# The memory term of an attention kernel as 64 more keys of its last score block

## The chip, the cores and the metric

The kernel runs on one core of one Trainium2 chip. The metric is the device time of the run in microseconds (us). Three runs of the kernel before took 566.57, 567.1 and 568.01 us, median 567.1. The engines are TensorE (PE, with its weight loads as PEld), VectorE (DVE), ScalarE (ACT), GpSimd (POOL) and SyncE (SP), which issues all DMAs here.

## The reference

For 4 batches, 8 heads, 576 positions and 64 channels, all in float32:

```
a     = exp(s - max(s)) / (sum + 1e-9),  s = q k^T / 8, causal
local = a v
phi(x) = max(x, 0) + exp(min(x, 0))
mem   = phi(q) M_prev / (phi(q) . z_prev + 1e-6)
out   = g * mem + (1 - g) * local,       g = sigmoid(beta), per head
x     = out as 2304 rows of 512
y     = ((x w1) * (x w2)) w3 w_out
```

Since nothing stands between w3 and w_out, the kernel multiplies these two once and uses their product.

## The kernel before, in words

The work goes by **pairs**: two heads (a = 0, 1) of one batch, 16 pairs in all, four to a batch. The 576 queries of a head are cut into five chunks: chunk 0 has 64 queries (those of both heads share one tile, `sm0`), chunks 1 to 4 have 128 each, for 64 + 128 c keys (`KE`). The scores of a chunk are a tile `sm{a}{c}` of 128 queries by `KE[c]` keys and 64 columns of zeros, so that whole blocks of 128 columns can be transposed.

A pair passes through these steps (names are the functions; lines are those of the profile):

- `s_all`, `s_mm0` (L205, L191): scores on TensorE; `s_red` (L182) on VectorE adds the mask and takes the maximum; `s_exp` (L215) on ScalarE; `s_norm` (L219 to L224) on VectorE divides by the sum and by the gate's part (1 - g, in `gis`).
- `t_mm` (L234, L255): transposes of the score blocks on TensorE into a PSUM bank `s`, copied by ScalarE into `pt` (L265). The groups are called 1, 2, h, 3a, 3b, 4a, 4b, 5.
- The memory term: `mem_a` (L138, L139, ScalarE) and `mem_b` (L144, VectorE) build phi(q) in the tile `qn`; GpSimd multiplies it by z (L146), VectorE sums over channels and makes n = g / sum (L151 to L157), GpSimd scales phi(q) by n (L159). `mem_t` (L165) transposes the five blocks and ScalarE copies them to `mt` (L167). `mem_mm` (L271, L272) multiplies `mt` by the memory matrix of both heads, which stand as diagonal blocks in `md`, into the PSUM tile `x`.
- `pv_mm` (L281): transposed scores times v are added to the same `x`; the two heads write the lower and the upper 64 partitions. v is five blocks of 128 keys; the last one holds 64 keys and 64 zeros.
- `fin` (L292, L293): `x` leaves PSUM as a high part and a remainder, the input of the MoE products.

Float32 matmuls stand in the trace as two records each.

Beside the pairs runs a **fill**: TensorE work that is cut into small steps and dealt out evenly over the F marks of the string `ORDER`, which also gives the order of a pair's steps. In batch 0 the fill is the product of w3 and w_out (L427), in batches 1 to 3 the MoE products of the batch before (`gemm1` L477, with L483 to L489 behind it; `gemm2` L497), and after the last pair those of the last batch, alone. The weights come as 64-bit floats; ScalarE and VectorE convert them in 40 jobs (`conv_tick`, L314 to L327): the first 24 are w_out and w3, the last 16 are w1 and w2 (`wp`, `wsp`). Their loads are `wst<-w_out`, `wst<-w3t` and `wst<-w`.

All loads are issued by SP in program order, and a DMA waits for the eighth DMA before it to land. The framework reorders instructions of an engine by priority before the program is built, so the order on an engine is not that of the code.

Of the kernel before, what the change touches and what calls it, by code (L numbers as in the profile page):

```python
# [13 lines left out]
ALU = mybir.AluOpType  # L14
# [7 lines left out]
    "lv mt t1 c c F "  # L22
# [3 lines left out]
    "t4b t5 F "  # L26
    "mm pv ma F "
# [15 lines left out]
def attention_moe_kernel(  # L43
# [22 lines left out]
    PT = 1920  # L66
# [27 lines left out]
    sm = [[None] + [const.tile([128, KE[c] + 64], F32, name=f"sm{a}{c}") for c in range(1, 5)] for a in range(2)]  # L94
    qd = const.tile([128, 128], F32, name="qd")
    md = const.tile([128, NC, 128], F32, name="md")
# [4 lines left out]
    raw_t, v_t, qn_t, z_t, mt_t, pt_t, sums_t, stat = ({} for _ in range(8))  # L101
# [13 lines left out]
    def load_v(p):  # L115
        b, h = heads(p)
        t = v_t[p] = v_p.tile([128, 2, 5, D], F32, tag="v", name="v")
        for a in range(2):
            nc.sync.dma_start(out=t[:, a], in_=v[b, h + a])

    def load_qn(p):
        b, h = heads(p)
        t = mem_p.tile([128, 5, 2, D], F32, tag="qn", name="qn")
        nc.sync.dma_start(out=t, in_=qn[b, h // 2])
        zt = z_p.tile([128, 2, D], F32, tag="z", name="z")
        zs = z_prev[b, h:h + 2]
        nc.sync.dma_start(out=zt, in_=bass.AP(tensor=zs.tensor, offset=zs.offset, ap=[[0, 128], [D, 2], [1, D]]))
        qn_t[p], z_t[p] = t, zt

    def load_m(b):  # L130
        src = m_prev[b].rearrange("d (j t) e -> d t j e", t=2)
        for a in range(2):
            nc.sync.dma_start(out=md[64 * a:64 * a + 64, :, 64 * a:64 * a + 64], in_=src[:, a])

    def mem_a(p):
        t = qn_t[p]
        e = mem_p.tile([128, 5, 2, D], F32, tag="e", name="e")
        nc.scalar.activation(out=e, in_=t, func=ACTF.Relu, scale=-1.0)  # L138
        nc.scalar.activation(out=e, in_=e, func=ACTF.Exp, scale=-1.0)  # L139
        stat["e", p] = e  # L140

    def mem_b(p):
        t, e = qn_t[p], stat["e", p]
        nc.vector.scalar_tensor_tensor(out=t, in0=t, scalar=0.0, in1=e, op0=ALU.max, op1=ALU.add)  # L144
        zb = z_t.pop(p).rearrange("p (o h) d -> p o h d", o=1).to_broadcast([128, 5, 2, D])
        nc.gpsimd.tensor_tensor(out=e, in0=t, in1=zb, op=ALU.mult)  # L146

    def mem_c(p):
        t, e = qn_t[p], stat.pop(("e", p))
        n = st_p.tile([128, 10, 1], F32, tag="n", name="n")  # L150
# [80 lines left out]
    def t_mm(p, what):  # L231
# [3 lines left out]
        if what in ("4a", "4b", "3a", "3b"):  # L235
# [28 lines left out]
        for s, d in jobs:
            nc.scalar.activation(out=d, in_=s, func=ACTF.Copy)  # L265
# [427 lines left out]
```

## Time and profile before

| | us |
|---|---|
| median of three runs (566.57 to 568.01) | 567.1 |
| span of the profiled execution | 564.3 |
| PE busy | 542.7 (96%) |
| PEld busy | 433.6 (77%) |
| DVE busy | 281.2 (50%) |
| ACT busy | 276.7 (49%) |
| POOL busy | 106.7 (19%) |

The span runs from the first to the last instruction of the profiled execution; a run's time has some 2.8 us more around it. Busy shares are means over stages with different limits; in the page's 40 slices VectorE is at 9 tenths in slices 2 and 6, TensorE in nearly all from slice 8 on. A matmul's end is modelled, so starts are the better measure.

### The profile page before, as it was taken

To read this page: it belongs to the slowest core of one execution; us is meant where nothing else is said; L and a number is where in the kernel's file an instruction comes from. 1 tells how busy PE (TensorE), PEld (TensorE's weight loads), DVE (VectorE), ACT (ScalarE), POOL (GpSimd) and SP (SyncE) were. 2 spreads that over 40 slices of the span, in tenths; PEclk is the share of its full clock that TensorE was granted. 3 is DMA by queue.
4 is the path that set the end of the run, shared out by engine and by line. 5 is a ranking of instruction groups with operands and counts; after the bars stand their busy time and mean duration, and the time that the engine had idled before them with its cause. 6 is when DMAs were issued, how large, how long until landed. Compare 5 with 4: busy or idle time off the path is not lost.

```text
span 564.3 us, 9257 instructions
## 1 busy us (share of the span) xinstructions
PE 542.7 (96%) x3440; PEld 433.6 (77%) x3440; DVE 281.2 (50%) x896; ACT 276.7 (49%) x723; POOL 106.7 (19%) x137
## 2 busy tenths in 40 slices
PE   4899989799999999999999999999999999999997
PEld 2344544458896979787978898798969797998995
DVE  6986899759653436263626272624534351111110
ACT  5656775749562637173725464354625361220210
POOL 1101202010430122212230313031301220220210
PEclk9899999999999999999999999999999999999999
DMA  7991646612111202121213021311112000000001
GB/s 294 417 375 51 218 132 224 208 49 94 40 62 44 87 28 69 57 88 30 67 29 106 28 55 35 100 48 39 58 43 88 23 2 20 20 1 37 1 1 56
DMA packets 23068, 48.31 MB, mean 86 GB/s; under 512 B 6896, under 2 KB 13040, under 8 KB 21488
## 3 DMA queue, kind: packets, MB, share of 16 engines
q1 hardware_dynamic: 23024, 47.72, 25.1%
q8 instruction: 27, 0.44, 0.3%
q14 instruction: 17, 0.14, 0.1%
HBM read 43.00 MB, written 4.72 MB: 85 GB/s over the span
## 4 chain that ended last, share of the span: by engine, by line
PE 83%; DVE 8%; ACT 4%; DMA 3%; issue 1%; SPq 0%; POOL 0%; DVEq 0%; ACTq 0%; POOLq 0%
PE m L477 37%; PE m L497 18%; PE s L234 8%; PE x L281 7%; PE s L205 5%; PE m L427 3%; DMA wst<-w 2%; PE x L272 2%; PE sx L205 2%; PE x L165 1%; ACT sm L215 1%; DMA wst<-w_out 1%; DVE sm L224 1%; DVE wsp L327 1%; ACT pt L265 1%; DVE w3s L319 1%
## 5 line engine op out<-in xcount | busy, mean ns | idle before, releaser
L477 PE MATMUL m<-xs,wsp 128*128 128x288 f32 x1536 | 223.5, 299 | 0.0
L477 PEld LDWEIGHTS m<-xs,wsp 128*128 128x128 f32 x1536 | 206.9, 188 | 1.2
L489 POOL TENSOR_TENSOR ht<-a,ht 128x288 fp32r<-128x288 f32 (+2 forms) x96 | 59.0, 628 | 261.6 <-ACT ht L488 242.3
L215 ACT ACTIVATE sm<-sm,mx 128x320 f32<-128x320 f32 (+3 forms) x144 | 82.6, 575 | 45.2 <-DVE mx L182 45.1
L497 PE MATMUL m<-wH,ht 128*128 128x512 f32 x288 | 95.4, 398 | 0.0
L265 ACT ACTIVATE pt<-s 128x512 f32<-128x512 f32 (+1 forms) x144 | 63.8, 497 | 27.7 <-PE s L234 27.4
L486 DVE SCALAR_TENSOR_TENSOR a<-m,a 128x288 f32<-128x288 f32 x64 | 29.2, 456 | 91.7 <-PE m L477 87.4
L427 PE MATMUL m<-wo,w3s 128*128 128x512 f32 x128 | 63.5, 625 | 5.7 <-DVE w3s L319 3.8
L234 PE MATMUL s<-ident,sm 128*128 128x128 f32 x448 | 61.7, 273 | 3.1 <-DVE sm L224 2.9
L497 PEld LDWEIGHTS m<-wH,ht 128*128 128x128 f32 x288 | 54.1, 188 | 11.5
L234 PEld LDWEIGHTS s<-ident,sm 128*128 128x128 f32 x448 | 52.3, 140 | 10.8 <-DVE sm L224 4.5
L488 ACT ACTIVATE ht<-a 128x288 fp32r<-128x288 f32 (+2 forms) x96 | 31.4, 361 | 56.0 <-DVE a L486 56.0
L182 DVE CUSTOM_DVE_ANT_0 sm<-s,mask 128x320 f32<-128x320 f32 (+3 forms) x112 | 45.7, 448 | 23.1 <-PE s L205 23.1
L497 PE MATMUL m<-wL,ht 128*128 128x512 f32 x144 | 56.2, 390 | 0.0
L224 DVE TENSOR_SCALAR sm<-sm,sums 128x320 f32<-128x320 f32 (+3 forms) x144 | 54.2, 430 | 1.1
L146 POOL TENSOR_TENSOR e<-qn,z 128x640 f32<-128x640 f32 x16 | 25.8, 1612 | 149.0 <-DVE qn L144 149.0
L483 ACT ACTIVATE a<-m 128x288 f32<-128x288 f32 x64 | 26.3, 411 | 47.7 <-PE m L477 42.2
L281 PEld LDWEIGHTS x<-pt,v 128*64 128x64 f32 x384 | 25.0, 137 | 29.9 <-issue 23.3
L281 PE MATMUL x<-pt,v 128*64 128x448 f32 (+4 forms) x384 | 46.7, 392 | 0.0
L293 DVE TENSOR_TENSOR xs<-x,xs 128x576 fp32r<-128x576 f32 x16 | 12.1, 755 | 66.0 <-ACT xs L292 66.0
L427 PEld LDWEIGHTS m<-wo,w3s 128*128 128x128 f32 x128 | 22.8, 197 | 28.1 <-issue 16.6
L205 PE MATMUL s<-raw 64*128 64x320 f32 (+3 forms) x256 | 38.1, 412 | 4.4 <-DMA raw<-qkt 4.4
(65 smaller groups left out, 458.0 us busy)
## 6 DMA issues: line engine op xcount, KB each, us to landing
raw<-qkt SPq DMA_DIRECT2D x16, 576.0 KB, 3.8
wst<-w3t SPq DMA_DIRECT2D x8, 1024.0 KB, 9.0
wst<-w SPq DMA_DIRECT2D x16, 512.0 KB, 4.7
qn<-qn SPq DMA_DIRECT2D x16, 320.0 KB, 3.0
v<-v SPq DMA_DIRECT2D x32, 160.0 KB, 2.3
out<-o SPq DMA_DIRECT2D x18, 256.0 KB, 2.0
wst<-w_out SPq DMA_DIRECT2D x4, 1024.0 KB, 12.1
z<-z_prev SPq DMA_DIRECT2D x16, 64.0 KB, 2.8
```

The lines of the kernel that those rows point to most:

```text
L182: nc.vector.tensor_tensor_reduce(out=sm[a][c][:, lo:hi] if c else sm0[:, 0:64], in0=x, in1=mask[:, S - KE[c] + lo:S - KE[c] + hi] if c els ...
L205: nc.tensor.matmul(y, lhsT=t[r, 0, 128 * c - 64:128 * c + 64], rhs=t[r, 1, lo:hi], start=True, stop=True)
L215: nc.scalar.activation(out=x, in_=x, func=ACTF.Exp, bias=mx, scale=-1.0, accum_out=sums_of(p)[:, k:k + 1])
L224: nc.vector.tensor_scalar(out=x, in0=x, scalar1=sums_of(p)[:, k:k + 1], scalar2=None, op0=ALU.mult)
L234: tr = lambda o, c, a, kc: nc.tensor.transpose(ps[:, o:o + 128], sm[a][c][:, 128 * kc:128 * kc + 128], ident)
L265: nc.scalar.activation(out=d, in_=s, func=ACTF.Copy)
L281: nc.tensor.matmul(x[64 * a:64 * a + 64, 384 + q0:384 + q1], lhsT=vv[:, a, kc], rhs=pt[:, a, o:o + q1 - q0], start=False, stop=(q0 == 0 or ...
L427: nc.tensor.matmul(ps, lhsT=w[:, 128 * kc:128 * kc + 128], rhs=wo[:, 512 * (kc % 2):512 * (kc % 2) + 512], start=(kc == 0), stop=(kc == 7))
L477: nc.tensor.matmul(ps[:, 0:U], lhsT=w[:, i, x, j], rhs=x_t[NC * b + j][:, xx, U * u:U * u + U], start=(k == 0), stop=(k == 11))
L488: nc.scalar.activation(out=hbuf(f, 0)[:, p:p + c], in_=a[:, o:o + c], func=ACTF.Copy)
L489: nc.gpsimd.tensor_tensor(out=hbuf(f, 1)[:, p:p + c], in0=a[:, o:o + c], in1=f32(hbuf(f, 0)[:, p:p + c]), op=ALU.subtract)
L497: nc.tensor.matmul(ps, lhsT=hbuf(f, a)[:, p:p + 128], rhs=b[f], start=(k == 0), stop=(k == 23))
```

## The change

The memory term becomes 64 more keys. Chunk c's last block of 128 score columns had 64 keys and 64 zeros; the zeros are replaced by phi(q) scaled by g / (phi(q) . z + 1e-6), 64 features for each query. v's block for that chunk has 64 rows of v below and the 64 rows of the memory matrix above, so one product adds both terms. As each chunk ends at another key, v gets nine blocks: four whole ones, and five (one for each chunk) of half v and half memory. `mem_t`, `mem_mm`, `load_m` and the tile `md` go; the score tiles of chunks 1 to 4 become slices of one tile `smx`, so that GpSimd can write two chunks of both heads in one instruction. The features are loaded in an order that fits the chunks (`qn` as nine blocks). The transposes are regrouped: 1, 2, h, 3a, 3b, 4a, 4b and s.

```diff
 ORDER = (
-    "lv mt t1 c c F "
+    "lv t1 c c F "
...
-    "t4b t5 F "
-    "mm pv ma F "
+    "t4b ts F "
+    "pv ma F "
...
     def load_v(p):
         b, h = heads(p)
-        t = v_t[p] = v_p.tile([128, 2, 5, D], F32, tag="v", name="v")
-        for a in range(2):
-            nc.sync.dma_start(out=t[:, a], in_=v[b, h + a])
+        t = v_t[p] = v_p.tile([128, 2, 9, D], F32, tag="v", name="v")
+        for a in range(2):
+            nc.sync.dma_start(out=t[:, a, 0:4], in_=v[b, h + a][:, 0:4])
+            nc.sync.dma_start(out=t[0:64, a, 4:9], in_=v[b, h + a][0:64])
+            m = m_prev[b][:, h + a]
+            nc.sync.dma_start(out=t[64:128, a, 4:9], in_=bass.AP(tensor=m.tensor, offset=m.offset, ap=[[DM, D], [0, 5], [1, D]]))
...
     def load_qn(p):
...
-        nc.sync.dma_start(out=t, in_=qn[b, h // 2])
...
+        nc.sync.dma_start(out=t[half[0], 0:8], in_=y[half[1], 0:4].rearrange("p t h d -> p (t h) d"))
+        nc.sync.dma_start(out=t[half[1], 0:8], in_=y[half[0], 1:5].rearrange("p t h d -> p (t h) d"))
+        for a in range(2):
+            nc.sync.dma_start(out=t[half[a], 8], in_=y[half[0], 0, a])
...
     def mem_b(p):
...
-        nc.gpsimd.tensor_tensor(out=e, in0=t, in1=zb, op=ALU.mult)
...
+        nc.gpsimd.tensor_tensor(out=by_pair(e), in0=by_pair(t), in1=zb, op=ALU.mult)
+        nc.gpsimd.tensor_tensor(out=e[:, 8], in0=t[:, 8], in1=zt[:, 2], op=ALU.mult)
...
     def mem_c(p):
...
-        nc.gpsimd.tensor_tensor(out=tv, in0=tv, in1=n.to_broadcast([128, 10, D]), op=ALU.mult)
-
-    def mem_t(p):
-        t = qn_t.pop(p)
-        x = ps_x.tile([128, 1024], F32, tag="x", name="x")
-        for i in range(5):
-            nc.tensor.transpose(x[:, 384 + 128 * i:512 + 128 * i], t[:, i].rearrange("p h d -> p (h d)"), ident)
-        mt = mt_t[p] = mem_p.tile([128, S], F32, tag="mt", name="mt")
-        nc.scalar.activation(out=mt, in_=x[:, 384:960], func=ACTF.Copy)
...
+        nc.gpsimd.tensor_tensor(out=sm0[:, 64:128], in0=t[:, 8], in1=n[:, 8].to_broadcast([128, D]), op=ALU.mult)
+        for k, lo, q in ((0, 0, 384), (4, 512, 640)):
+            d = smx[:, :, lo:lo + 2 * q].rearrange("p a (k q) -> p k a q", q=q)[:, :, :, q // 2 if k == 0 else 576:]
+            d = d[:, :, :, 0:D]
+            by_pair = lambda y: y[:, k:k + 4].rearrange("p (k a) d -> p k a d", a=2)
+            nc.gpsimd.tensor_tensor(out=d, in0=by_pair(t), in1=by_pair(n).to_broadcast([128, 2, 2, D]), op=ALU.mult)
...
+            blocks, lo, st, o = {
+                "1": (((1, 0), (1, 1)), 0, SP[1], 0),
+                "2": (((2, 0), (2, 1)), 0, 384, 128),
+                "s": (((2, 2), (4, 4)), 1024, 384, 256),
+            }[what]
...
-    def mem_mm(p):
-        x = stat["x", p] = ps_x.tile([128, 1024], F32, tag="x", name="x")
-        mt = mt_t.pop(p)
-        lhsT = md[:, p % NC]
-        nc.tensor.matmul(x[:, 384:512], lhsT=lhsT, rhs=mt[:, 0:128], start=True, stop=False)
-        nc.tensor.matmul(x[:, 512:960], lhsT=lhsT, rhs=mt[:, 128:576], start=True, stop=False)
-
     def pv_mm(p):
-        x, pt, vv = stat["x", p], pt_t.pop(p), v_t.pop(p)
-        for kc in range(5):
-            off = 1024 if kc == 4 else 576 * kc
-            for q0, q1 in ((0, 128), (128, 576)) if kc == 0 else ((128 * kc, 576),):
-                for a in range(2):
...
+        x = stat["x", p] = ps_x.tile([128, 1024], F32, tag="x", name="x")
+        pt, vv = pt_t.pop(p), v_t.pop(p)
+        jobs = [(kc, 512 * kc, 128 * kc + 64, 576) for kc in range(4)]
+        jobs += [(4 + c, SP[c], max(128 * c - 64, 0), 128 * c + 64) for c in (1, 2, 3, 4, 0)]
+        for k, o, q0, q1 in jobs:
             for a in range(2):
...
+                nc.tensor.matmul(
+                    x[64 * a:64 * a + 64, X0 + q0:X0 + q1], lhsT=vv[:, a, k], rhs=pt[:, a, o:o + q1 - q0],
+                    start=k in (0, 4), stop=k in (8, 4),
+                )
...
-    for c in range(1, 5):
-        for a in range(2):
-            nc.vector.memset(sm[a][c][:, KE[c]:KE[c] + 64], 0.0)
...
     for b in range(B):
-        load_m(b)
```

The order of the instructions on TensorE, from the last transposes of the first pair of batch 1 to its value products, before (L234 transposes, L477 fill, L271 and L272 memory products, L281 value products):

```order
L477 MATMUL m<-xs,wsp 128x288 x9
L234 MATMUL s<-ident,sm_115 128x128 x4
L234 MATMUL s<-ident,sm_111 128x128
L234 MATMUL s<-ident,sm_115 128x128
L477 MATMUL m<-xs,wsp 128x288 x12
L271 MATMUL x<-mt,md 128x128
L272 MATMUL x<-mt,md 128x448
L281 MATMUL x<-pt,v 64x128 x2
L281 MATMUL x<-pt,v 64x448 x4
L281 MATMUL x<-pt,v 64x320 x2
L281 MATMUL x<-pt,v 64x192 x2
L281 MATMUL x<-pt,v 64x64 x2
```

The same place now (L240 transposes, L468 fill, L272 value products):

```order
L240 MATMUL s<-ident,smx 128x128 x7
L468 MATMUL m<-xs,wsp 128x288 x9
L240 MATMUL s<-ident,smx 128x128 x5
L468 MATMUL m<-xs,wsp 128x288 x12
L272 MATMUL x<-pt,v 64x512 x2
L272 MATMUL x<-pt,v 64x384 x2
L272 MATMUL x<-pt,v 64x256 x2
L272 MATMUL x<-pt,v 64x128 x10
L272 MATMUL x<-pt,v 64x64 x2
```

The value products follow the fill directly, as 18 instructions instead of 12 and two.

SP's queue before, from the features of pair 1 to the second load of w1 and w2:

```order
L124 DMA qn<-qn 128x640
L127 DMA z<-z_prev 128x128
L303 DMA wst<-w 128x1024
L113 DMA qd<-qkt 64x64 x2
L119 DMA v<-v 128x320 x2
L303 DMA wst<-w 128x1024
```

SP's queue now, from pair 1's values to the first two loads of w1 and w2; ahead of the rows stand pair 1's features and pair 2's scores' inputs:

```order
L123 DMA v<-v 128x256
L124 DMA v<-v 64x320
L126 DMA v<-m_prev 64x5x64
L133 DMA qn<-qn 64x512
L134 DMA qn<-qn 64x512
L136 DMA qn<-qn 64x64 x2
L139 DMA z<-z_prev 128x128
L142 DMA z<-z_prev 64x64 x2
L294 DMA wst<-w 128x1024 x2
```

Both weight loads moved behind pair 1's values and pair 2's features.

VectorE before, from the conversion of the first halves of w1 and w2 (`wp`, `wsp`) to the reductions of pair 2's scores (ISA):

```order
L318 TENSOR_SCALAR wp<-wp 128x512
L327 TENSOR_TENSOR wsp<-wp,wsp 128x512
L151 TENSOR_REDUCE n<-e 128x10
L319 SCALAR_TENSOR_TENSOR wp<-wst,wp 128x512
L293 TENSOR_TENSOR xs<-x,xs 128x576
L419 SCALAR_TENSOR_TENSOR wL_129<-m,wH_121 128x512
L182 ISA sm_109,mx<-s,mask 128x320
```

VectorE now, among the same reductions, the first six rows of which stand ahead of these:

```order
L188 ISA smx,mx<-s,mask 128x192
L188 ISA mx 128x1
L164 TENSOR_REDUCE n<-e 128x9
L309 TENSOR_SCALAR wp<-wp 128x512
L165 TENSOR_SCALAR n<-n 128x9
L310 SCALAR_TENSOR_TENSOR wp<-wst,wp 128x512
L188 ISA smx,mx<-s,mask 128x448
```

Two whole conversions stood ahead of pair 2's reductions; now the first one begins between them. Up to pair 3's last normalisation eight of these conversions stood on VectorE, now seven.

## Rows read from the trace of the kernel before

**Rows 1.** Stages: busy us (count) of PE, PEld, DVE, ACT, POOL; clock, DMA.
```profile
core 0: us, PE busy (x) PEld busy (x) DVE busy (x) ACT busy (x) POOL busy (x), PEclk, DMA share, GB/s
...
70.00:90.00 20.00, 17.46 (x82) 9.71 (x82) 19.78 (x60) 16.47 (x41) 2.83 (x2) 1.00 0.53 174
90.00:110.00 20.00, 16.44 (x76) 8.17 (x73) 18.26 (x58) 11.25 (x29) 1.55 (x1) 1.00 0.64 213
...
130.00:564.30 434.30, 430.18 (x2944) 374.51 (x2943) 177.40 (x577) 192.10 (x522) 89.92 (x118) 1.00 0.15 46
```

**Rows 2.** Waits of PE, longest first: us in total, times, longest.
```profile
PE s L205 <- DMA raw<-qkt: 4.4, 1, 4.4
```

**Rows 3.** Timeline of PE: start, us, instruction, idle time before it.
```profile
81.02 1.32 PE L234 MATMUL s<-ident,sm 128*128 128x128 f32 x10 [1.14 <-DVE sm L224]
...
108.56 1.32 PE L234 MATMUL s<-ident,sm 128*128 128x128 f32 x10 [1.75 <-DVE sm L224]
```

**Rows 4.** The chain that ended last: start, us, what; pair 3, then pair 4.
```profile
114.54 0.22 PE x L271 x2
114.77 0.75 PE x L272 x2
115.52 2.85 PE x L281 x24
...
128.69 0.55 PE x L165 x5
```

**Rows 5.** Timeline of PE in narrow windows over one pair's value products.
```profile
200.76 0.33 PE L281 MATMUL x<-pt,v 128*64 128x128 f32 x2
...
200.92 0.66 PE L281 MATMUL x<-pt,v 128*64 128x128 f32 x4
...
202.54 0.44 PE L281 MATMUL x<-pt,v 128*64 128x320 f32 x2
...
203.07 0.50 PE L281 MATMUL x<-pt,v 128*64 128x192 f32 x4
...
203.40 0.28 PE L281 MATMUL x<-pt,v 128*64 128x64 f32 x4
```

**Rows 6.** Groups by line and form: busy us, mean ns, idle before.
```profile
L281 PEld LDWEIGHTS x<-pt,v 128*64 128x64 f32 x384 | 25.0, 137 | 29.9 <-issue 23.3 <-DMA z<-z_prev 1.3 <-DMA wst<-w 0.7
```

**Rows 7.** Timelines of PE and of POOL around one pair's last transposes.
```profile
197.84 0.81 PE L234 MATMUL s<-ident,sm 128*128 128x128 f32 x6
...
195.78 1.56 POOL L146 TENSOR_TENSOR e<-qn,z 128x640 f32<-128x640 f32 x1 [1.62 <-DVE qn L144]
198.95 0.40 POOL L489 TENSOR_TENSOR ht<-a,ht 128x96 fp32r<-128x96 f32 x1 [1.61 <-ACT ht L488]
199.31 1.26 POOL L159 TENSOR_TENSOR qn<-qn,n 128x640 f32<-128x640 f32 x1
```

**Rows 8.** Timeline of SP: issues at the start.
```profile
4.30 0.48 SPq L590 DMA_DIRECT2D beta_sb<-beta  x1
...
7.05 1.30 SPq L388 DMA_DIRECT2D wst<-w_out  x3
```

**Rows 9.** DMA issues: KB each, median us from issue to landing.
```profile
v<-v SPq DMA_DIRECT2D x32, 160.0 KB, 2.3
...
wst<-w_out SPq DMA_DIRECT2D x4, 1024.0 KB, 12.1
...
beta_sb<-beta SPq DMA_DIRECT2D x1, 4.0 KB, 8.6
```

**Rows 10.** Groups by line and form: the conversion of w1 and w2, VectorE.
```profile
L327 DVE TENSOR_TENSOR wsp<-wp,wsp 128x512 fp32r<-128x512 f32 x16 | 14.2, 894 | 3.1 <-ACT wsp L326 3.0
...
L319 DVE SCALAR_TENSOR_TENSOR wp<-wst,wp 128x512 uint32<-128x512 uint32 x16 | 10.8, 683 | 0.2
...
L318 DVE TENSOR_SCALAR wp<-wp 128x512 uint32<-128x512 uint32 x16 | 7.6, 482 | 1.6 <-ACT wp L314 1.6
```

**Rows 11.** The chain in the first 62 us.
```profile
54.66 5.25 DMA wst<-w
```

More of the change, by code (lines that the diff above doesn't have):

```diff
@@ L65, in attention_moe_kernel @@
     KE = [64, 192, 320, 448, 576]
-    PT = 1920
+    PT = 1856
+    SP = [1792, 896, 1280, 1408, 1664]
+    X0 = 448
     XT = 7
@@ L93, in attention_moe_kernel @@
     sm0 = const.tile([128, 128], F32, name="sm0")
-    sm = [[None] + [const.tile([128, KE[c] + 64], F32, name=f"sm{a}{c}") for c in range(1, 5)] for a in range(2)]
+    smx = const.tile([128, 2, 1792], F32, name="smx")
+    SO = [None, 0, 256, 640, 1152]
+    sm = [[None] + [smx[:, a, SO[c]:SO[c] + KE[c] + 64] for c in range(1, 5)] for a in range(2)]
+    gs = const.tile([128, NC, 9], F32, name="gs")
     qd = const.tile([128, 128], F32, name="qd")
-    md = const.tile([128, NC, 128], F32, name="md")
     wH = [const.tile([128, DM], F32R, name=f"wH{i}") for i in range(NF)]
     wL = [const.tile([128, DM], F32R, name=f"wL{i}") for i in range(NF)]
-    raw_t, v_t, qn_t, z_t, mt_t, pt_t, sums_t, stat = ({} for _ in range(8))
+    raw_t, v_t, qn_t, z_t, pt_t, sums_t, stat = ({} for _ in range(7))
     def heads(p):
@@ L148, in mem_c @@
+        nc.gpsimd.tensor_tensor(out=e[:, 8], in0=t[:, 8], in1=zt[:, 2], op=ALU.mult)
     def mem_c(p):
-        t, e = qn_t[p], stat.pop(("e", p))
-        n = st_p.tile([128, 10, 1], F32, tag="n", name="n")
-        nc.vector.tensor_reduce(out=n, in_=e.rearrange("p t h d -> p (t h) d"), axis=AX.X, op=ALU.add)
+        t, e = qn_t.pop(p), stat.pop(("e", p))
+        n = st_p.tile([128, 9, 1], F32, tag="n", name="n")
+        nc.vector.tensor_reduce(out=n, in_=e, axis=AX.X, op=ALU.add)
         nc.vector.tensor_scalar(out=n, in0=n, scalar1=1e-6, scalar2=None, op0=ALU.add)
@@ L264, in t_mm @@
[L264 to L284 removed]
+            s = 256 if c == 4 else 0
@@ new lines, in t_mm @@
+            o = 128 if c == 4 else 256
+            d = pt[:, a, s:s + 1536].rearrange("p (k q) -> p k q", q=384)[:, :, o:o + 128]
+            job = (ps.rearrange("p (k q) -> p k q", q=128), d)
+        elif what == "h":
+            nc.tensor.transpose(ps[:, 0:128], sm0, ident)
+            job = (ps[:, 0:128].rearrange("p (a q) -> p a q", a=2), pt[:, :, SP[0]:SP[0] + 64])
+        else:
+            blocks, lo, st, o = {
[3 more added lines that the diff above has]
+            }[what]
+            for a in range(2):
+                for i, (c, kc) in enumerate(blocks):
+                    tr(256 * a + 128 * i, c, a, kc)
+            d = pt[:, :, lo:lo + 2 * st].rearrange("p a (k q) -> p a k q", q=st)[:, :, :, o:o + 128]
+            job = (ps.rearrange("p (a k q) -> p a k q", a=2, q=128), d)
@@ L559, in pair_step @@
             th=(1, lambda: t_mm(p, "h")),
-            t5=(1, lambda: t_mm(p, "5")),
+            ts=(1, lambda: t_mm(p, "s")),
             ss=(nx, lambda: s_all(p + 1)),
@@ L598, in attention_moe_kernel @@
     make_identity(nc, ident)
-    nc.gpsimd.memset(md, 0.0)
     for a in range(2):
         nc.vector.memset(qd[64 * a:64 * a + 64, 64 - 64 * a:128 - 64 * a], 0.0)
-    for c in range(1, 5):
-        for a in range(2):
-            nc.vector.memset(sm[a][c][:, KE[c]:KE[c] + 64], 0.0)
-    nc.vector.memset(sm0[:, 64:128], 0.0)
     with tc.high_priority(1000):
@@ L618, in attention_moe_kernel @@
     gp = gi.rearrange("p (j a) -> p j a", a=2)
-    for k in range(4):
-        nc.vector.tensor_copy(out=gis[:, :, 2 * k:2 * k + 2], in_=gp)
-    for a in range(2):
-        nc.vector.tensor_copy(out=gis[64 * a:64 * a + 64, :, 8], in_=gp[64 * a:64 * a + 64, :, a])
+    gq = g_sb.rearrange("p (j a) -> p j a", a=2)
+    for y, yp in ((gis, gp), (gs, gq)):
+        for k in range(4):
+            nc.vector.tensor_copy(out=y[:, :, 2 * k:2 * k + 2], in_=yp)
+        for a in range(2):
+            nc.vector.tensor_copy(out=y[64 * a:64 * a + 64, :, 8], in_=yp[64 * a:64 * a + 64, :, a])
     s_exp(0, 2)
```

59 lines of the change are left out of this document (15 added, 44 removed).

## The prediction

> **What bounds the kernel now.** I read the stages first. In the long stage from 130 us to the end [rows 1] the first pair of columns, TensorE, is busy 430.18 of 434.30 us at the full granted clock (1.00, the 2.4 GHz level), while VectorE has 177.40, ScalarE 192.10 and GpSimd 89.92. In the two stages before 110 us it is otherwise: VectorE is busy 19.78 of 20 us and 18.26 of 20, TensorE only 17.46 and 16.44. Next the waits of TensorE: the longest in the whole execution is 4.4 us, for the first load [rows 2], and the late ones, at 81.02 and 108.56 us, are for VectorE's normalised scores [rows 3]; after 108.56 none is listed. So there are two regimes: up to about 110 us (pairs 0 to 2, counting from 0, and the weight conversion) VectorE and the loads set the pace; from pair 3 on (13 of the 16 pairs) whatever TensorE no longer does comes off the end. The chain of waits says the same: from there on it runs on TensorE alone, with a pair's pieces in it [rows 4].
>
> **The change part by part.** The profiled execution has a span of 564.3 us; the three timed runs have a median of 567.1, so 2.8 us lie around the span. I subtract from the span and add 2.8.
>
> *A. Five transposes of the scaled features go.* The chain has them as one piece of 0.55 us for x5 [rows 4]. The score transposes stay at 29 a pair: two blocks that stood half empty now carry features, the four that were spread over two groups form one. Gain 0.55 us a pair.
>
> *B. The two memory products go* (128 and 448 columns): 0.22 + 0.75 = 0.97 us a pair in the chain [rows 4].
>
> *C. The value products grow.* Before: 12 instructions a pair, 1600 columns for each of two heads. After: 18 instructions, 512 + 384 + 256 + 128 + 4 x 128 + 64 = 1856 columns. Each instruction stands in the trace as two records, and the two heads' records run side by side. From the starts in [rows 5]: the four 320-wide records of a head pair begin at 202.54 and the 192-wide ones follow at 203.07, so one pass of both heads takes 0.53 / 2 = 0.265 us (0.83 ns a column); the 192-wide ones take (203.40 - 203.07) / 2 = 0.165 us (0.86 ns a column). 256 more columns x 2 records x 0.85 ns = 0.44 us. The difference of the two paces is worth about 0.006 us for a record pair, and there are 6 more instructions a pair, hence 6 more pairs of heads' records: 0.04. Cost 0.47 us. Ends: 0.43 if only columns count; for the narrow instructions the dearest row is the first 128-wide one, whose second record starts 0.16 us after the first (200.92 - 200.76) where 128 x 0.85 = 0.11 is the pace; ten record pairs are now 128 wide, 10 x 0.05 = 0.5 more, so 0.97 at worst. I take 0.47, as the first one also opens a new kind of work, and the 64-wide records at the end keep the pace.
>
> The rule that speaks against this: the Trainium skill, TensorE: Matmul & The Clock Gate, Part 3, The mechanism, says that a weight load overlaps running matmuls only if it is for another group of rows (beside a background buffer that the same page names); all of these use all rows. Here a load takes 25.0 us / 384 = 0.065 us of busy time [rows 6]; two such loads laid bare would make the 192-wide step 0.165 + 0.13 us. The trace shows 0.165, which the columns alone account for, so it does not agree. It is the fourth rival below.
>
> Net a pair: 0.55 + 0.97 - 0.47 = 1.05 us (ends 0.55 and 1.09). For the 13 pairs 3 to 15: 13.7 us (7.2 to 14.2).
>
> *D. The other engines in that regime.* ScalarE loses a 576-wide copy and one narrow copy a pair, VectorE a tenth of each feature step: at nothing, since TensorE covers both. GpSimd gets five instructions for two. Now 1.56 + 1.26 = 2.82 us [rows 7]; the elements fall from 1280 to 1152 and three more starts come, each below the 0.40 us of a whole 96-wide one, so 2.8 to 4.0 us a pair. New is what they wait for: they write into the score blocks, so those of the next pair wait until this pair's transposes are read. In the trace these end at 198.65 and GpSimd's scaling begins at 199.31 anyway [rows 7], and the next pair's transposes come only after that pair's scores. At nothing; behind the waiting instruction stand GpSimd's remainders of h, for which ScalarE and the last products wait (third rival).
>
> *E. The loads.* Values, features and norms take 13 DMAs a pair instead of 4, all on SP, and the memory matrix comes with every pair. An issue costs SP about 0.48 us, a landing some 2.3 us [rows 8, 9], and every DMA waits for the eighth before it. 16 x 0.48 = 7.7 us of issue in a pair's period of 108.56 - 81.02 = 27.5 us [rows 3]: hidden. Were they to go one at a time, 16 x (0.48 + 2.3) = 44 us, they would not be; eight in flight say that they don't.
>
> *F. The first 110 us.* Three effects. First, TensorE's own 3 x 1.05 = 3.2 us for pairs 0 to 2. Second, the order of VectorE: before pair 3's last normalisation stand eight converted halves of w1 and w2, now seven; one costs 0.48 + 0.68 + 0.89 = 2.05 us [rows 10]. Also the wait for the weight load of 54.66 us (5.25 us, [rows 11]) no longer stands before pair 1's copies, as these loads are issued later. Together between 2.05 (VectorE alone decides) and 5.2 (both); I take 4.0. Third, a loss at the start: three w_out loads were issued at 7.05 us; now they follow a feature load and norms that must wait for the landing of beta's load, issued at 4.30 and landing 8.6 us later, 12.9 us [rows 8, 9]. The DMA engines were filled with earlier loads meanwhile, and the loads took a median of 12.1 us from issue: issued late they wait less behind others. Between 0 and 5.9 us; I take 1.5, nearer to the end at which the engines just have other work. Net gain 4.0 - 1.5 = 2.5 us (ends -3.9 and 5.2).
>
> *Sum.* 13.7 + 2.5 = 16.2 us: 564.3 - 16.2 = 548.1 us of span, and 550.9 us for the median run.
>
> **The rivals.**
> 1. *The start and the weight loads take the early gain back.* SP issues the first load of w1 and w2 now behind pair 1's values and pair 2's features; if VectorE idles for it and the conversion then falls into the time in which the first MoE products want it, the early net is -3.9 and another 2.05 us x 2 of conversion shows as waits of TensorE around 130 to 150 us. 13.7 - 3.9 - 4.1 = 5.7: 561.4 us. For it: VectorE has no air from 70 to 110 us. Against: from 130 us on it is busy 41% of the time.
> 2. *More in the first part.* If VectorE, freed of two conversions before pair 2's scores as the order shows, lets TensorE use all the idle time of 70 to 110 us, 2.54 + 3.56 = 6.1 us [rows 1], and the start costs nothing: 13.7 + 6.1 = 19.8, 547.3 us; with the cheaper PV 546.8.
> 3. *Slower: GpSimd as a gate.* The writes into the score blocks stand in GpSimd's queue waiting for the pair's last transposes, and the remainders of h behind them; ScalarE's next copy of a product waits for the buffer that the remainder reads, and TensorE for that copy. It decides once the stall is over 16.2 / 12 = 1.35 us in each of the 12 pairs that have MoE work beside them. If GpSimd's whole 2.8 us lie open each time: 12 x 2.8 = 33.6, less 16.2: 584.5 us. Against: GpSimd is busy a fifth of its time in that stage and the transposes are done 0.66 us before it needs them.
> 4. *Weight loads in the open*: 12 more records a pair x 0.065 = 0.78 us more, net 0.27 a pair, 13 x 0.27 + 2.5 = 6.0: 561.1 us. The steps in [rows 5] are against it. It is what the rule under C comes to.
>
> **How the numbers follow.** Forecast 0.70 (546 to 556 us, its own range: PV's ends and the early ends moved singly). Rival 1 0.12, rival 2 0.10, rival 3 0.04, rival 4 0.04. The range: from 545.5, below rival 2, to 558, where PV at its dear end (7.2 + 2.5 = 9.7: 557.4) lies inside and the full rivals 1, 3 and 4 outside, some 0.17. Less than 0.3% (1.7 us) is about what a measurement of this kernel can't tell from no change. Faster: all but rival 3 and a part of rival 1 gone worse: 0.94; within 0.3%: 0.02; slower: 0.04.
>
> **What would show it.** After: five groups of 0.55 us and the memory products gone from the chain; the value products at 3.3 us instead of 2.85 (3.8 would be the dear end, 4.1 rival 4); TensorE busy in all of the time from pair 3's transposes, and those at 104 to 106 us instead of 108.56; no wait of TensorE on GpSimd over 0.3 us. Wrong if TensorE's waits after 110 us sum to several us, if the narrow value products keep a step over 0.13 us, or if pair 3's transposes begin after 110 us.

## The result, and the profile after

The changed kernel takes 569.28 us (median of 9 runs), the kernel before 566.57 us beside it. The ratio is 1.0054, with a 95% interval of 1.0036 to 1.0072: slower by half a per cent. 550.9 us was forecast, and the range ended at 558. Runs more than 1.5% above the fastest of their kernel are left out of all medians and ratios here; there was one, 563.31 us, among the four of c2 below.

The removed work is gone. The chain of waits has no feature transposes and no memory products any more, and the value products stand in it with the length that was forecast, 3.3 us (2.85 before, [rows 4]). Chain of the kernel after (start, us, what):

```profile
243.02 3.29 PE x L272 x36
```

So the time must have come in elsewhere. Stages of the kernel after (length; busy us and count of PE, PEld, DVE, ACT, POOL; granted clock; DMA share; GB/s), against [rows 1]:

```profile
70.00:90.00 20.00, 18.05 (x106) 10.74 (x105) 15.40 (x53) 14.47 (x36) 3.43 (x5) 1.00 0.52 157
90.00:110.00 20.00, 18.61 (x89) 9.52 (x88) 15.86 (x41) 13.00 (x30) 4.12 (x5) 1.00 0.77 237
110.00:130.00 20.00, 17.53 (x103) 10.11 (x102) 16.64 (x47) 12.26 (x28) 4.24 (x5) 1.00 0.58 168
130.00:150.00 20.00, 14.50 (x76) 12.33 (x76) 14.26 (x42) 13.96 (x36) 1.98 (x3) 0.83 0.39 122
150.00:568.70 418.70, 412.21 (x2925) 361.86 (x2923) 165.08 (x561) 177.40 (x482) 91.56 (x149) 1.00 0.18 52
```

The kernel before in the two stages from 110 us:

```profile
110.00:130.00 20.00, 20.00 (x102) 11.18 (x101) 10.75 (x41) 12.41 (x34) 2.80 (x2) 1.00 0.23 71
130.00:150.00 20.00, 20.00 (x154) 17.54 (x155) 15.19 (x31) 13.70 (x30) 6.57 (x5) 1.00 0.20 63
```

Before, VectorE was busy 19.78 us of the stage from 70 to 90 us; now it has 15.40 there and converts more of the weights later: from 110 to 130 us it is busy 16.64 us, before 10.75. In the 40 us in which TensorE had no gap it is now busy 17.53 + 14.50 = 32.0 us, and in the second half of them the granted clock is 0.83 as well.

The best measure is when each pair's value products begin. Against the kernel before, from both timelines of TensorE: pair 0 +3.0 us, pair 1 +7.2, pair 2 +3.3, pair 3 +2.9, pair 4 +11.5, pair 5 +13.9; from there it falls in every pair, to +4.4 in pair 15. The ten pairs from 5 to 15 gain 9.5 us, 0.95 each where 1.05 was forecast. All of the loss, 13.9 us, lies before pair 5, and 8.6 us of it between pair 3 and pair 4. Pair 4's value products in TensorE's timeline, before and after:

```profile
141.03 2.92 PE L281 MATMUL x<-pt,v 128*64 128x128 f32 x24
```

```profile
152.54 3.36 PE L272 MATMUL x<-pt,v 128*64 128x512 f32 x36
```

Two places stand out on the chain, and both are in-order queues.

*SP's queue.* Chain of the kernel after, pair 1 to 2:

```profile
61.00 3.29 DMA v<-v
64.30 0.46 POOL e L159
...
67.00 1.20 POOL smx L173 x2
...
68.21 0.47 SPq L133
...
71.80 0.59 SPq L142
...
72.44 5.02 DMA wst<-w
...
77.48 0.67 ACT wp L305
78.15 1.88 ACT smx L221 x7
```

The chain goes through a load of values, the feature norms, GpSimd's write of the features into the score blocks (which frees the one feature buffer), then seven small loads of the next features and z, issued one behind another in 4.2 us, and only then a load of w1 and w2, for which ScalarE waits with softmax exponentials behind it. In the kernel before a first such load was issued at 39.47 us, ahead of pair 1's values at 53.61 (below). Pair 1's own lag, +7.2, is not of this load: its value products begin at 71.58 us, before the load is issued.

*ScalarE's queue.* Chain of the kernel after, pair 4:

```profile
123.80 7.08 DMA v<-v
...
130.89 2.22 DMA qn<-qn
...
133.19 0.69 ACT e L148
...
135.11 1.31 ACT smx L221 x4
...
140.69 1.97 PE s L240 x8
```

The features here (L148, L149) are those of pair 5; the exponentials (L221) behind them are pair 4's. ScalarE stood 2.15 us waiting for the features' DMA, worked on them for 1.4 us, and pair 4's exponentials, VectorE's normalisation and TensorE's transposes came behind. TensorE stood idle for 5.5 us before these transposes, and the granted clock was 0.50 for 5.5 us from them on (last section). Waits of the kernel after, longest first, of the whole execution (us in total, times, longest):

```profile
ACT e L148 <- DMA qn<-qn: 35.4, 11, 4.6
...
PE s L240 <- DVE smx L230: 10.9, 4, 5.5
...
PE s L240 <- POOL smx L173: 0.5, 1, 0.5
```

Most of the 35.4 us come later, when MoE products cover them (TensorE is busy 412.21 of the last 418.70 us); the wait at 133 us had no cover.

In the kernel before, ScalarE did not wait for features at all: they had their place behind copies of transposed weights, as its ScalarE timeline shows:

```profile
109.27 1.43 ACT L265 ACTIVATE pt<-s 128x512 f32<-128x512 f32 x4 [1.85 <-PE s L234]
110.56 0.76 ACT L138 ACTIVATE e<-qn 128x640 f32<-128x640 f32 x1
```

There the feature buffer was freed by TensorE's feature transposes, for which SP waited 8.3 us in 4 waits from 40 to 150 us. Now GpSimd's write into the score blocks frees it, and the framework puts the next features ahead of the exponentials. Why it does so is argued from the order alone; that the order costs the time is what the runs below test.

### The profile page after: what moved, and what is told of

Read it like the earlier page. It is cut to its first block, busy times and chain, and to the rows that moved or that the text cites. A ratio compares the mean times of both kernels' runs of the same rounds, so it can differ in the third digit from the quotient of the medians.

```text
span 568.7 us, 9657 instructions
## 1 busy us (share of the span) xinstructions
PE 537.4 (95%) x3488; PEld 432.3 (76%) x3488; DVE 277.6 (49%) x893; ACT 267.7 (47%) x691; POOL 114.3 (20%) x184
## 2 busy tenths in 40 slices
DMA packets 39582, 52.00 MB, mean 91 GB/s; under 512 B 21360, under 2 KB 29552, under 8 KB 38000
## 4 chain that ended last, share of the span: by engine, by line
PE 74%; DMA 6%; DVE 5%; issue 5%; ACT 4%; POOL 2%; SPq 2%; POOLq 0%; DVEq 0%; ACTq 0%
PE m L468 32%; PE m L488 18%; PE s L240 7%; PE x L272 7%; PE s L211 4%; PE m L418 4%; DMA wst<-w 2%; PE sx L211 2%; DMA v<-v 2%; ACT smx L221 2%; DVE smx L188 1%; POOL smx L173 1%; DMA qn<-qn 1%; DVE smx L230 1%; ACT pt L263 1%
## 5 line engine op out<-in xcount | busy, mean ns | idle before, releaser
L468 PE MATMUL m<-xs,wsp 128*128 128x288 f32 x1536 | 225.9, 301 | 1.3 <-DVE a L477 1.1
L468 PEld LDWEIGHTS m<-xs,wsp 128*128 128x128 f32 x1536 | 208.6, 189 | 4.2 <-DVE a L477 1.6
L221 ACT ACTIVATE smx<-smx,mx 128x320 f32<-128x320 f32 (+3 forms) x128 | 77.4, 606 | 42.8 <-DVE mx L188 42.6
L477 DVE SCALAR_TENSOR_TENSOR a<-m,a 128x288 f32<-128x288 f32 x64 | 29.2, 456 | 118.7 <-PE m L468 116.0
L240 PE MATMUL s<-ident,smx 128*128 128x128 f32 x448 | 63.3, 279 | 11.5 <-DVE smx L230 10.9
L240 PEld LDWEIGHTS s<-ident,smx 128*128 128x128 f32 x448 | 53.7, 143 | 22.3 <-DVE smx L230 14.1
L488 PEld LDWEIGHTS m<-wH,ht 128*128 128x128 f32 x288 | 54.1, 188 | 11.5
L272 PE MATMUL x<-pt,v 128*64 128x128 f32 (+4 forms) x576 | 57.0, 341 | 0.3 <-ACT pt L263 0.2
L230 DVE TENSOR_SCALAR smx<-smx,sums 128x320 f32<-128x320 f32 (+3 forms) x128 | 55.1, 480 | 1.0
L272 PEld LDWEIGHTS x<-pt,v 128*64 128x64 f32 x576 | 36.1, 137 | 24.3 <-issue 17.2
L158 POOL TENSOR_TENSOR e<-qn,z 128x512 f32<-128x512 f32 x16 | 21.3, 1330 | 139.8 <-DVE qn L154 92.1
L188 DVE CUSTOM_DVE_ANT_0 smx<-s,mask 128x320 f32<-128x320 f32 (+2 forms) x96 | 42.1, 486 | 6.2 <-PE s L211 6.2
L211 PE MATMUL s<-raw 64*128 64x192 f32 (+3 forms) x256 | 39.2, 414 | 4.4 <-DMA raw<-qkt 4.4
```

What stands on the lines that cost most here:

```text
L188: nc.vector.tensor_tensor_reduce(out=sm[a][c][:, lo:hi] if c else sm0[:, 0:64], in0=x, in1=mask[:, S - KE[c] + lo:S - KE[c] + hi] if c els ...
L211: nc.tensor.matmul(y, lhsT=t[r, 0, 128 * c - 64:128 * c + 64], rhs=t[r, 1, lo:hi], start=True, stop=True)
L221: nc.scalar.activation(out=x, in_=x, func=ACTF.Exp, bias=mx, scale=-1.0, accum_out=sums_of(p)[:, k:k + 1])
L230: nc.vector.tensor_scalar(out=x, in0=x, scalar1=sums_of(p)[:, k:k + 1], scalar2=None, op0=ALU.mult)
L240: tr = lambda o, c, a, kc: nc.tensor.transpose(ps[:, o:o + 128], sm[a][c][:, 128 * kc:128 * kc + 128], ident)
L272: nc.tensor.matmul(x[64 * a:64 * a + 64, X0 + q0:X0 + q1], lhsT=vv[:, a, k], rhs=pt[:, a, o:o + q1 - q0], start=k in (0, 4), stop=k in (8, 4),
```

## The experiments

Each is given by its edit, its expectation and its time; the kernel before beside them took 566.46 to 566.66 us. The last columns say how much later (+) or earlier (-) than in the kernel before the value products of a pair begin, from TensorE's timelines of the profiled executions. Each column is thus one execution's: those of a1, d3 and d5 took 2.2 to 2.7 us more than the median in the table, that of e2 2.3 us less. c2's trace is not used.

| kernel | us | ratio to before, 95% | pair 0 | pair 1 | pair 3 | pair 5 | pair 15 |
|---|---|---|---|---|---|---|---|
| changed kernel | 569.28 | 1.0036-1.0072 | +3.0 | +7.2 | +2.9 | +13.9 | +4.4 |
| a1_all_merged | 563.56 | 0.9930-0.9971 | +1.3 | +6.9 | +6.8 | +7.5 | +0.2 |
| a2_feat_merged | 566.57 | 0.9976-1.0010 | +0.7 | +5.3 | +6.0 | +6.6 | +0.3 |
| a3_vals_merged | 563.17 | 0.9924-0.9957 | +3.1 | +6.1 | +1.5 | +5.5 | -4.1 |
| a4_before_split | 570.95 | 1.0061-1.0091 | +3.3 | +6.2 | +5.3 | +5.3 | +5.3 |
| c2_merged_pin | 556.78 | 0.9785-0.9865 | | | | | |
| c4_merged_pin_early | 552.84 | 0.9745-0.9774 | +1.6 | +3.2 | -2.0 | -3.3 | -12.6 |
| c6_after_pin_early | 563.85 | 0.9936-0.9966 | +3.1 | +7.2 | +4.3 | +6.4 | -3.0 |
| c7_after_early | 568.31 | 1.0005-1.0038 | +3.2 | +7.3 | +6.3 | +12.0 | +3.1 |
| d3_count | 558.02 | 0.9834-0.9867 | +2.1 | +6.5 | +1.1 | +3.6 | -5.8 |
| d4_packets | 556.76 | 0.9814-0.9843 | +1.5 | +3.4 | +2.0 | +0.7 | -8.7 |
| d5_start | 551.16 | 0.9709-0.9761 | -1.9 | -0.1 | -2.0 | -3.4 | -12.7 |
| d6_after_early3 | 562.51 | 0.9913-0.9956 | +2.9 | +7.6 | +3.9 | +5.4 | -4.0 |
| e1_after_qn2 | 558.84 | 0.9857-0.9910 | +2.3 | +6.4 | +2.3 | +1.7 | -7.7 |
| e2_after_poolq | 560.43 | 0.9868-0.9918 | +0.7 | +5.6 | +2.7 | +1.4 | -8.0 |

**Is it the number of loads?** The host lays the arrays out so that features, z and each head's values with memory come in one DMA each; the tiles keep their contents.

```diff
-        for a in range(2):
-            nc.sync.dma_start(out=t[:, a, 0:4], in_=v[b, h + a][:, 0:4])
-            ...
+        for a in range(2):
+            nc.sync.dma_start(out=t[:, a], in_=v[b, h + a])        # a1, a3
...
-        nc.sync.dma_start(out=t[half[0], 0:8], in_=...)
-        ...
+        nc.sync.dma_start(out=t, in_=qn[b, h // 2])                # a1, a2
+        nc.sync.dma_start(out=zt, in_=...)                         # a1, a2
```

> The changed kernel with the same bytes in the same tiles, but 4 DMAs a pair in place of 13 (features in one, z in one, values and memory of a head in one each; the host lays the arrays out so). Theory 1 (the count of DMAs in SP's in-order queue brings features and weights late): the 14 us lost by pair 5 come back, 552 us (548 to 557), and TensorE's busy time in 130-150 us is near 20 us instead of 14.5. Theory 2 (the small packets of 256 B slow the DMA engines): the same time, since they go too. Theory 3 (a feature buffer that comes free late, or the changed order of the conversions, whatever the loads): 563 to 570 us.

> Only the features and z are merged (2 DMAs instead of 7); values and memory keep their 6, with nearly all the packets of 256 B. Theory 1: 8 DMAs a pair instead of 13, and the features no longer end a train of seven: 555 us (551 to 560). Theory 2 (small packets): 566 us or more, since most of them stay. Theory 3: 563 to 570 us.

> Only the values and the memory are merged (2 DMAs instead of 6); the features and z keep their 7. Theory 1: 9 DMAs a pair, about half of the loss comes back: 560 us (555 to 564). Theory 2 (small packets): 553 us, since 640 of about 770 small packets a pair go. Theory 3: 563 to 570 us.

a4 cuts the loads of the kernel before instead, four a pair in its code (one for each head's values, one for the features, one for z): values into three a head, features into four, z into three.

> The kernel before with its 5 loads of a pair cut into 13 (values 6, features 4, z 3), same bytes, no other edit. Theory 1: the loads alone cost what the changed kernel lost, 578 us (572 to 584). Theory 2: few packets get smaller than 256 B but many more of them: 570 us or less. Theory 3: 566 to 568 us, as before.

Theories 1 and 2 failed as the main cause. With as many loads as before, and fewer small packets, a1 still had lost 7.5 us by pair 5 in its profiled execution. TensorE was busy 19.07 us from 130 to 150 us there, as theory 1 wanted, but only 14.54 from 110 to 130: the gap came a pair earlier. And 13 loads put on the kernel before cost it 4.4 us (5.3 in the profiled execution, all of it by pair 3), not 14, which fits none of the three. Only theory 3's band held a1; a2 lies in those of theories 2 and 3, a3 in those of theories 1 and 3, so these two decide nothing. So the loads are some 4 to 6 us of the loss (a4, a1), and something else is more. In a1's trace it could be seen without the loads' noise. ScalarE's timeline of a1 (start, us, instruction, idle time before):

```profile
104.24 0.44 ACT L210 ACTIVATE smx<-smx,mx 128x192 f32<-128x192 f32 x1
...
107.12 0.68 ACT L137 ACTIVATE e<-qn 128x576 f32<-128x576 f32 x1 [2.35 <-DMA qn<-qn]
...
109.39 0.65 ACT L210 ACTIVATE smx<-smx,mx 128x448 f32<-128x448 f32 x1
```

TensorE's of a1:

```profile
103.68 6.23 PE L407 MATMUL m<-wo,w3s 128*128 128x512 f32 x14
115.46 1.97 PE L229 MATMUL s<-ident,smx 128*128 128x128 f32 x8 [5.56 <-DVE smx L219]
```

And SP's of a1, then of the kernel before:

```profile
52.68 0.80 SPq L123 DMA_DIRECT2D v<-v  x2
53.52 0.91 SPq L283 DMA_DIRECT2D wst<-w  x2
```

```profile
39.47 0.42 SPq L303 DMA_DIRECT2D wst<-w  x1
52.38 1.13 SPq L113 DMA_DIRECT2D qd<-qkt  x2
53.61 1.00 SPq L119 DMA_DIRECT2D v<-v  x2
```

Pair 1's values wait for the buffer that pair 0's value products still read, and the first load of w1 and w2 stands behind them instead of ahead.

**Is it the place in the queue?** Two edits put back the order of the kernel before:

```diff
-        nc.scalar.activation(out=job[1], in_=job[0], func=ACTF.Copy)
+        stat["ptc"] = nc.scalar.activation(out=job[1], in_=job[0], func=ACTF.Copy)
...
-            ma=(nx, lambda: mem_a(p + 1)),
+            ma=(nx, lambda: mem_a_pinned(p + 1)),      # issued after stat["ptc"]
...
     def conv_tick():
+        if k == 14:
+            load_upto(25)                              # the first w12 load
```

> The kernel with 4 merged loads a pair, and one more edit: the two ScalarE operations of the next pair's features are held behind the last copy of this pair's transposed weights on ScalarE (their place in the kernel before), so that they no longer stand ahead of the softmax exponentials of the larger chunks and wait there for the features' DMA (2.35 us at 107 us, after which TensorE waited 5.6 us). Theory 4 (the place of an operation in an engine's in-order queue, ahead of its late DMA, makes the loss): the loss at pair 3 goes, 559.5 us (557 to 561.5). Theory 5 (VectorE bounds the first 110 us, busy 19.3 of 20 us in 70-90, so ScalarE's and SP's order changes nothing): 562.5 to 565 us.

> As c2_merged_pin, and the first w12 load is put ahead of the values of pair 1 in SP's queue again (it was issued at 53.5 us there behind values that waited for their buffer, at 39.5 us in the kernel before; the exponentials behind its conversion on ScalarE came 5.6 us later than before). Theory 4: the loss at pair 1 goes too (it is some 5 us at the value products of pair 1), 556 us (553 to 559). Theory 5: 562 to 565 us.

> The changed kernel with its 13 loads a pair, with both edits of order: features held behind the copies of the transposed weights on ScalarE, the first w12 load ahead of the values of pair 1. Theory 4: the wait of ScalarE for the features and with it TensorE's 5.5 us at 140 us go, 560 us (556 to 564). Theory 5, or if the issue of 13 loads decides by itself: 567 to 570 us.

> The changed kernel with the first w12 load ahead of the values of pair 1 in SP's queue (72.4 us in the changed kernel), nothing else. Theory 4: 565 us (562 to 567), some of the loss at pair 1 comes back, the features still block ScalarE at 133 us. Theory 5: 567 to 570 us.

This settles the main cause. In the merged kernel the first edit alone gave 6.8 us between medians (of three runs, 554.06 to 558.97 us), both gave 10.7 us: 552.84 us. Both times lie 0.2 us under theory 4's bands, so the gain was a little more than forecast. No byte and no operation differs between a1 and c4, only the order; theory 5's 562 to 565 us is excluded for it. The same first load was issued at 40.50 us, the features stood behind the copies, and TensorE was busy in all of the 20 us in which the changed kernel had 17.53. ScalarE's timeline of c4, then TensorE's, then its stage:

```profile
106.15 0.78 ACT L214 ACTIVATE smx<-smx,mx 128x576 f32<-128x576 f32 x1
109.01 2.73 ACT L256 ACTIVATE pt<-s 128x512 f32<-128x512 f32 x6 [1.98 <-PE s L233]
...
113.28 0.68 ACT L137 ACTIVATE e<-qn 128x576 f32<-128x576 f32 x1
```

```profile
108.30 1.10 PE L233 MATMUL s<-ident,smx 128*128 128x128 f32 x8 [2.54 <-DVE smx L223]
```

```profile
110.00:130.00 20.00, 20.00 (x117) 12.07 (x116) 12.85 (x48) 13.60 (x36) 2.98 (x5) 1.00 0.40 108
```

With the 13 loads the edits helped less: 5.4 us both (c6, at the end of its band), and the early load alone 1.0 us, which is theory 5's band and a miss for theory 4: with the features still ahead on ScalarE, an earlier weight load buys little (the intervals of c7 and the changed kernel overlap). The lag of pair 1 needs both: with the early load it stays at +6.4 or more where SP issues 13 loads (c6, c7, d3, d6, e1), and falls to +3.4 or less only where they are 4 a pair (c4, d4, d5). 11.0 us stay between c6 and c4, whose code differs in the loads alone.

**What the 13 loads cost, once the order is right.** d3 and d4 start from c4. d3 cuts its four loads by partitions, d4 reads the values from rows with a gap; d5 moves the first features; d6 starts from c6 and loads three weights early.

```diff
+            for r in (slice(0, 64), slice(64, 96), slice(96, 128)):       # d3
+                nc.sync.dma_start(out=t[r, a], in_=v[b, h + a][r])
...
+            nc.sync.dma_start(out=t[:, a], in_=v[b, h + a][:, :, 0:D])     # d4, rows of 2 D
...
-    load_qn(0)                                                            # d5
     load_raw(6)
+    load_qn(0)
...
-            load_upto(25)                                                 # d6
+            load_upto(27)
```

> The merged kernel with both edits of order (552.8 us), its 4 loads a pair cut by partitions into 13: the same bytes in the same packets, 13 DMAs. Theory 1 (the count in SP's in-order queue): most of the 11 us between it and the changed kernel with the same edits (563.9 us) come back as a loss, 560 us or more. Theory 2 (small packets): 552 to 555 us.

> The merged kernel with both edits of order, the values and the memory of a head still in one DMA, but read from rows that leave a gap, so in packets of 256 B (1152 a head instead of 128 of 2304 B). Theory 1: 552 to 555 us. Theory 2 (small packets): 558 us or more.

> The merged kernel with both edits of order, the first features and z loaded behind the three w_out loads instead of ahead of them. Theory: the start's loss (1.6 us at the first value products) goes, 551 us (549.5 to 552.5). Rival: the first features are then late for the first pair and the time stays or grows, 552.5 to 555 us.

> The changed kernel with 13 loads a pair, features held behind the copies, and three w12 loads (not one) ahead of the values of pair 1. Theory 4 (what stands ahead of the w12 loads in SP's queue is most of what is left): 558 us (556 to 561). Theory 1 (the 13 loads themselves): 562.5 to 564.5 us, as with one.

Both theories hold a part, and neither time lies in a band. 13 DMAs in place of 4 cost 5.2 us with the data cut into the same packets (the trace of d3 counts 2,529 packets more than that of c4, nearly all under 512 B), and 256 B packets cost 3.9 us with the number of DMAs unchanged. But d4 has 41,360 packets under 512 B against 4,496 in c4, and the changed kernel 21,360, so its own share should be less: scaled by the packets added, 1.8 us (an estimate). In d4 the values land in 6.2 us (median) instead of 3.9, and issuing can take longer as well: at the start the issue of the same two loads took 7.27 us (at 29.09 us in d4) and 1.72 us (at 30.01 us in c4).

d3 and d4 got their own orders from the framework, so a part of either may be order again. d6 missed theory 4: two more early weight loads gave 1.3 us, at the very edge of the band of the count.

The Trainium skill, DMA: Bandwidth & Descriptors, Rules for kernel authors, says to coalesce many small transfers, and of two transfers to disjoint halves of the partitions not to bother, as they serialise. d3's 5.2 us agree with it in sign.

d5's gain at the start is real: 3.6 us earlier than c4 in pair 0, and pair 3's transposes still begin 2.8 us earlier (105.46 us against 108.30). TensorE's timeline of d5:

```profile
105.46 1.97 PE L233 MATMUL s<-ident,smx 128*128 128x128 f32 x8 [3.08 <-DVE smx L223]
```

By pair 3's value products the two are level (113.41 us against 113.50). What lies between is the granted clock: in this execution it was 0.50 from 106 to 111 us, in c4's it was 1.00, and the eight transposes took 1.97 us instead of 1.10. The other three runs of d5 took 550.15 to 552.03 us at a mean clock of 0.990 to 0.993, this one 553.34 at 0.985. The medians differ by 1.7 us, the spans of the two profiled executions by 0.1, the intervals overlap: not told apart.

**The number, or what waits at the head of the queue?** e1 gives features and z a second buffer; e2 issues their seven loads from GpSimd's queue. Both start from c6.

```diff
-    z_p = pool("z")
+    z_p = pool("z", 2)                                      # e1
+    qn_p = pool("qn", 2)
...
-        nc.sync.dma_start(out=t[half[0], 0:8], in_=...)     # e2, and the other six
+        nc.gpsimd.dma_start(out=t[half[0], 0:8], in_=...)
```

> The changed kernel with 13 loads a pair and both edits of order (563.9 us), features and z with two buffers instead of one, so that their loads don't stand in SP's queue until GpSimd has written the last features into the score blocks. Theory 6 (the wait for the one feature buffer at the head of SP's queue is what keeps the weights behind it late): 559 us (556 to 561). Rival (the 13 loads take their time in the queue whenever they come): 562 to 565 us.

> The changed kernel with 13 loads a pair and both edits of order, the 7 loads of features and z issued from GpSimd's queue instead of SP's: the same DMAs and packets, but SP's queue has 6 a pair and no wait for the feature buffer. Theory 1 (SP's in-order queue, its count and its waits): 557 us (554 to 560). Rival (the DMA engines themselves, by packets or by the count of DMAs whatever the queue): 562 to 566 us.

The second buffer gave 5.0 us: 558.84, inside theory 6's band. SP's waits from 40 to 150 us in c6 list those for the two buffers, features (L133) and z (L139):

```profile
SPq L133 <- POOL smx L177: 9.1, 4, 3.5
SPq L139 <- POOL e L163: 6.0, 2, 4.3
```

In e1 the first is gone and the second is 3.1 us, once; SP waits 13.4 us in 3 waits for the values' buffer instead, 1.6 in c6. Weight loads go out earlier. SP's timeline of c6, where four features stand between the first load and the next, then of e1:

```profile
84.11 0.58 SPq L298 DMA_DIRECT2D wst<-w  x1
87.09 0.47 SPq L133 DMA_DIRECT2D qn<-qn  x1
...
89.57 7.28 SPq L298 DMA_DIRECT2D wst<-w  x4
```

```profile
83.63 1.53 SPq L299 DMA_DIRECT2D wst<-w  x3
```

So the framework also gave SP's queue another order; which part of the 5.0 us is the wait and which this order was not separated.

The same 13 loads with the same packets thus cost 6.0 us over c4 and not 11.0; the other 5.0 go with the single buffers of features and z. The other queue gave 3.4 us, 0.4 short of theory 1's band and outside the rival's. It takes seven loads and their waits out of SP's queue and yet gave less than the second buffer; its features land later (median 4.0 us against 2.8 for the larger ones). So a part of the cost is SP's queue, and how much is the DMAs wherever they are issued stays open. The Trainium skill, DMA: Bandwidth & Descriptors, Issuing engines are not separate DMA queues, says that issuing from several engines saves only the issuing time. Nothing here contradicts it: seven issues took some 4 us of SP in the chain of the kernel after, in each pair, and e2 gained 3.4 us in all. In the traces the gain does not grow from pair to pair: 2.3 us at pair 0, which are gone again at pair 2, then 5.0 us from pair 4 on (+6.9 to +1.8). That what is saved is the wait of other loads in the queue fits this, but is not shown.

Fastest of all are c4 and d5, 552.84 and 551.16 us, 2.4% and 2.7% under the kernel before.

## Why the prediction was wrong

**A, B and C were right.** The chain holds 3.29 us for the value products against 3.3 forecast, the feature transposes and memory products are gone, and from pair 5 each pair gains 0.95 us (1.05 forecast). The fourth rival, weight loads in the open, would have shown 4.1 us; it is out.

**E failed: "hidden".** The step compared SP's issue time with a pair's period, 7.7 us with 27.5, an average. The queue is in order, and what counts is what stands at its head and who waits behind. The kernel before could have warned of it. Its SP waits from 40 to 150 us:

```profile
SPq L127 <- POOL e L146: 25.8, 5, 10.1
SPq L303 <- DVE wp L319: 24.6, 12, 4.4
SPq L113 <- PE s L191: 12.4, 1, 12.4
```

With four shorter groups they sum to 81 of 110 us: the queue, which the w1 and w2 loads share, stood at a buffer most of the time. Such waits are not a loss by themselves: over the same stretch SP's waits sum to 53 us in the changed kernel and to 83 us in c4, the faster one. They cost where something urgent stands behind. With the changed kernel's order the first weight load is issued 33 us later than before (72.44 against 39.47). Of the 16.4 us between the changed kernel and c4, 5.4 us go with the two edits of order (c6), 5.0 us with the single buffers of features and z (e1), 6.0 us with the loads as they are then left (c4 against e1). In the merged kernel, where the order is the only difference, it is worth 10.7 us; so the shares depend on the order in which they are taken.

**D failed in a place it did not look at.** "At nothing, since TensorE covers both" summed ScalarE's busy time; it has less of it now. But its features moved ahead of the exponentials and waited there for a DMA, 35.4 us in 11 waits, where the kernel before had none. GpSimd's writes, costed at nothing, hardly hold up TensorE (0.5 us in all; one wait, a little over the 0.3 us of the test), so the third rival is out; but they became what releases the features' loads.

**F had the right size for a kernel that keeps its order, and the wrong sign for this one.** Forecast was 2.5 us gained by pair 3; c4 and d5 have 2.0 at its value products. That c4's number is so near is partly luck: its transposes of pair 3 begin at 108.30 us, hardly before the 108.56 of the kernel before and not at 104 to 106. d5, without the loss at the start, has them at 105.46 and then loses to the clock. The changed kernel has 2.9 us lost at pair 3. The start's loss was given as 1.5 us: 3.0 in the changed kernel, 1.6 in c4. Of the 4.0 us that the rest of F was to gain, nothing shows: the lag is 3.0 at pair 0 and 2.9 at pair 3. The test written down beforehand caught it: the transposes of pair 3 begin after 110 us. TensorE's timeline of the kernel after:

```profile
113.34 1.11 PE L240 MATMUL s<-ident,smx 128*128 128x128 f32 x8 [2.29 <-DVE smx L230]
```

**Rival 1 named the place** (weight loads behind pair 1's values and pair 2's features, TensorE waiting from 130 to 150 us) and was given 0.12 and 561.4 us. It stopped at two late conversions, 4.1 us, and did not follow the exponentials that stand behind a late conversion or a late feature on ScalarE; 7.9 us were missing. (The chances of rivals 1, 3 and 4 add up to 0.20, not to some 0.17.)

**Left open:** why the framework put the features ahead (seen, not tested), how the 6.0 us divide between number, packets and the order that the framework makes of them, how e1's 5.0 us divide between the wait and SP's new order, and c2's exact size. A second buffer for the values, the other load that waits at SP's head, was not tried.

## What to carry to other kernels

A change that takes work off the busiest engine can move the release of a buffer, and with it the place of loads and small operations in in-order queues; read the new order on every queue for what stands ahead of a late DMA, not only the busy times. A load is hidden only if nothing behind it in its queue is urgent: look at its worst wait at the head and at what stands behind, not at its issue time against the period. When data needs another layout, change it once outside or in one DMA; thirteen pieces cost this kernel 11 us with single buffers for features and z, and 6 us with two.

## What the runs showed of the hardware

The same eight transposes of pair 3 or 4 took 1.10 to 1.11 us where the granted clock was 1.00, the 2.4 GHz level (c4 at 108.30 us, changed kernel at 113.34), and 1.97 us where it was 0.50, the 1.2 GHz level (changed kernel at 140.69 us, a1 at 115.46, d5 at 105.46). In the last three the clock fell while TensorE stood idle, for 5.50, 5.56 and 3.08 us. In the changed kernel it then stayed low for 5.5 us of work (length; busy us and count of PE, PEld, DVE, ACT, POOL; granted clock; DMA share; GB/s):

```profile
140.69:146.20 5.51, 5.51 (x25) 5.49 (x26) 5.32 (x14) 2.45 (x5) 0.00 (x0) 0.50 0.08 18
```

At half the rate that is some 2.8 us of lost work (an estimate), beside the wait of 5.5 us; together they make 8.3 of the 8.6 us by which the lag grows from pair 3 to pair 4. The length of the idle time alone does not tell when the clock falls: in c6 it fell after an idle time of 2.43 us, when TensorE was already at work again (a mean clock of 0.68 from 88 to 89 us), and in c4 it stayed at 1.00 after 2.54 us. Within one kernel it is a part of the spread: a1's runs took 561.22 us at a mean clock of 0.994 and 566.65 us at 0.981.
